# Attention and token-mixing MLP in one kernel: another tile for the fetched reciprocals, division in halves, fetches at other slots, one more raw weight block

## The chip, the cores and the metric

The kernel runs on one core of one Trainium2 chip. The metric is the device time of one execution in microseconds, as the median of several runs; lower is better. The profile is of one further execution, taken by the hardware profiler.

## What is computed

One input x (2048 tokens, 512 channels, float32) goes through two branches that a gate mixes.

```python
g = sigmoid((x * gate_w).sum(-1, keepdims=True))
# branch A: 32 heads of 16 channels
q, k, v = heads(x @ wqkv)
o = softmax(q @ k.T * 16**-0.5) @ v
a = merge(o) @ wo
# branch B: an MLP over the token axis, the same for every channel
h = layernorm(x)
u = gelu(einsum("bsd,sf->bdf", h, w1) + b1)       # F = 1792
b = einsum("bdf,fs->bds", u, w2) + b2             # transposed back to (tokens, channels)
out = g * a + (1 - g) * b
```

## The kernel before

**Precision.** Products are made of float32r parts: a matrix is split into a high part (a cast) and a low part (the difference), and three products are added (high by high, high by low, low by high). `split` (L66 the cast, L67 the subtraction) does this for weights, activations and the attention's result.

**First part, up to about 305 us.** Values, queries and keys are projected; q and k parts go to DRAM. Then comes the first layer of branch B, with w1 in blocks of 128 x 512. `load_weight` asks for a raw block on the SP queue (L132, tile `w_raw`, three buffers), and `split_weight` splits an earlier one. The second layer's blocks (w2) use the same tiles.

**Attention.** There are 32 *groups*: 16 pairs of heads, for the first half of the queries and then for the second. A group has 4 *slots* (the variable `two` counts all 128 of them), and a slot has 2 *phases*. In a phase TensorE makes 8 score products into PSUM banks (L830), ScalarE takes the exponentials (L850), and TensorE multiplies those of the phase before by the values (L788, 32 small matmuls). VectorE adds the result to the group's tile `ot` (L808), after which the bank is free again. `ot` holds for each head 16 rows of sums and one row with the sum of the exponentials.

**Work beside it.** The same phases carry 6 (at times 8) matmuls of other work (L894): the second layer of branch B, whose output rows L514 writes to DRAM, and the output projection by wo, in pieces. A table `dense` says which matmuls lie in which slot; a table `calls` says which functions are called at the start of a slot. Both are filled ahead of the loop (L694 to L711), with `at` as the slot that the schedule has reached.

**The way of a group's result.** After a group's last addition `store_sums` stores the 16 rows per head (L756, `o<-ot`, four stores), inverts the row of sums in two steps on VectorE (L762 a maximum, L763 a reciprocal), in place in `ot` until `open_end` has been called and afterwards in a tile `sums`, and stores the reciprocals (L769, `r<-...`). Once four groups are stored, `fetch_o` brings them back as one operand of 128 partitions: it reads the result into the low parts' tile (L614, `o_lo<-o`, 512 KB) and the reciprocals, each row repeated 16 times, into a tile `o_sum` (L615, `o_sum<-r`, 512 KB). Two slots later VectorE multiplies the two over all 1024 columns (L618) and, in the next free phase, splits the product into `o_hi` and `o_lo`. There are eight fetches: `fetch_o(0, 0..3)` for the first half of the queries, with `o_sum` (one buffer) in the pool `o_pool`, and `fetch_o(1, 0..3)`, with `o_sum` (one buffer) in the pool `end`.

**The list `slow`.** VectorE's work that has no fixed place stands in this list with the slot from which it may run. In each phase at most one entry is taken, ahead of the phase's scores.

**Output rows.** `project` multiplies a piece of the attention's result by wo. `load` (L632) reads the row that it is added to, one slot ahead; when the slot's matmuls end, L636 adds into it, and L656 (`out_dram<-row`) or L658 stores it. In slots 112 to 119 these are the final rows of the first half. In slots 120 to 127 they are `base` rows of the second half, which stay in place for the end.

**Last pair.** The last pair of heads doesn't go through DRAM. Its part of wo (`wq`) is read by four strided reads (L595) into a cleared tile `wq_raw` and split on VectorE, all from `open_end` at slot 112, the split from slot 117.

**Queues.** All these reads and stores are issued by SP, in program order. Each of them also waits until the one eight places ahead has landed, because eight semaphores are used in turn. The order inside attention is fixed by hand (`manual_schedule`); ahead of it a scheduler sets the order.

Of the kernel before, what the change touches and what calls it, by code (L numbers as in the profile page):

```python
# [10 lines left out]
F32 = mybir.dt.float32  # L11
# [4 lines left out]
ALU = mybir.AluOpType  # L16
AX = mybir.AxisListType
# [5 lines left out]
P = 128  # L23
S = 2048
D = 512
F = 1792
H = 32
DH = 16
# [3 lines left out]
NB = 512  # L32
# [23 lines left out]
LEAST_SUM = 1e-35  # L56
# [3 lines left out]
def gated_mix(ctx: ExitStack, tc: tile.TileContext, a_x, a_wqkv, a_wo, b_w1, b_b1, b_w2, b_b2, gate_w, out):  # L60
    nc = tc.nc
    xf, of = (t.rearrange("b s d -> (b s) d") for t in (a_x, out))

    def split(hi, lo, src, copy, sub):

        copy(hi, src)  # L66
        return sub(lo, src, hi.bitcast(F32), ALU.subtract)  # L67
# [15 lines left out]
    ident = const.tile([P, P], F32, name="ident")  # L83
# [17 lines left out]
    wk = wk_ctx.enter_context(tc.tile_pool(name="wk", bufs=3, side="right"))  # L101
# [19 lines left out]
    def load_weight():  # L121
        if blocks:
            src = blocks.pop(0)
            raw = wk.tile([P, NB], F32, name="w_raw", bufs=3)
            if len(src.shape) == 2:
                raw = raw[:, : src.shape[1]]
                dst = raw
            else:
                raw = raw[:, : src.shape[1] * P]
                dst = raw.rearrange("p (k s) -> p k s", s=P)  # L130
            with tc.issue_after(x_load.ins):
                nc.sync.dma_start(dst, src)  # L132
            loaded.append(raw)
# [281 lines left out]
    with tc.tile_pool(name="ln1", bufs=3, side="right") as ln, tc.tile_pool(name="gl", bufs=2, side="right") as gl:  # L415
# [29 lines left out]
        for f0, cs in order.items():  # L445
            n = min(NB, F - f0) // P
# [29 lines left out]
    o_pool = ctx.enter_context(tc.tile_pool(name="o", bufs=1, reuse_waits="tile"))  # L476
# [3 lines left out]
    QW = 2 * NB  # L480
# [64 lines left out]
    wq = []  # L545
# [30 lines left out]
    least = []  # L576
    rows = {}

    def open_end():

        nonlocal end, sums_of
        u_ctx.close()
        wk_ctx.close()
        end = end_ctx.enter_context(tc.tile_pool(name="end", bufs=1, side="right", reuse_waits="tile"))

        sums_of = end.tile([P, P], F32, name="sums_of")
        nc.vector.tensor_copy(
            sums_of.rearrange("p (j r) -> p j r", r=32),
            ident.rearrange("p (j r) -> p j r", r=32)[:, :, DH:VC].broadcast_to([P, P // 32, 32]),
        )  # L590
        wq.extend(end.tile([P, 2, D], F32R, name=f"wq{n}") for n in range(2))
        raw = end.tile([P, 2, D], F32, name="wq_raw")
        nc.gpsimd.memset(raw, 0.0)
        for j in range(4):
            nc.sync.dma_start(  # L595
                raw[32 * j : 32 * j + DH], a_wo[(H - 2) * DH : H * DH, :].rearrange("(i r) c -> r i c", i=2)
            )
        slow.append((two + 5, lambda: split(wq[0], wq[1], raw, nc.vector.tensor_copy, nc.vector.tensor_tensor)))

        least.append(end.tile([P, 1], F32, name="least"))  # L600
        nc.vector.tensor_reduce(least[0], ident.rearrange("p (j r) -> p j r", r=32)[:, :, DH], axis=AX.X, op=ALU.add)
        nc.vector.tensor_scalar(least[0], least[0], -1.0, 3e38, ALU.add, ALU.mult)
        nc.vector.tensor_scalar_add(least[0], least[0], LEAST_SUM)

    def fetch_o(half, k, pairs=4):

        n = pairs * 2
        assert stored.issuperset(half * NP + 4 * k + p for p in range(pairs))
        pool, name, bufs = (end, str(k), 1) if half else (o_pool, "", 2)
        rb = pool.tile([P, QW], F32, name="o_sum", bufs=1)[: n * DH]  # L610
        hi = pool.tile([P, QW], F32R, name=f"o_hi{name}", bufs=bufs)[: n * DH]
        lo = pool.tile([P, QW], F32R, name=f"o_lo{name}", bufs=bufs)[: n * DH]
        raw = lo.bitcast(F32)
        nc.sync.dma_start(raw, o_d[half][k][: n * DH])  # L614
        nc.sync.dma_start(rb, r_d[half][k][:n, None, :].broadcast_to([n, DH, QW]))  # L615

        at = two + (1 if two + 2 == NG * TWOS else 2)
        slow.append((at, lambda: nc.vector.tensor_mul(rb, raw, rb)))  # L618
# [59 lines left out]
    def call(at, *what):  # L678
        calls.setdefault(at, []).append(what)
# [397 lines left out]
```

## Time and profile before

| what | value |
|---|---|
| median of 3 runs | 1310.69 us (1309.16 to 1312.59) |
| profiled execution | 1314.28 us |
| its span, from the first to the last instruction | 1312.5 us |
| granted TensorE clock, mean | 0.99 |
| HBM traffic | 98.85 MB read, 35.78 MB written |

How to read the views that follow. The page gives the busy time of each engine. A table of stages gives, for stretches of time, the busy time of each engine with the number of instructions, the granted clock, the busy share of the 16 DMA engines and GB/s. A list of waits names who waited, at which line, for whom, with total, number and longest. A timeline row gives start, length, engine, line and operation, the tiles (output, then inputs), how many such instructions it merges, and in brackets the idle time before it with what ended it. The rows of an engine called SPq are the issues of transfers: their length is the time that issuing took, not the transfer. Rows of groups by form give count, busy us, mean ns and idle time before.

### The profile page before, as it was taken

What the parts mean: (1) busy time and instruction counts of PE and PEld (TensorE: products, weight loads), DVE (VectorE), ACT (ScalarE), POOL (GpSimd) and SP (SyncE); (2) the same over time, 40 slices, a digit from 0 to 9 for tenths busy, and PEclk for the clock granted to TensorE, in tenths of its full rate; (3) what the DMA queues carried; (4) which work ended last, traced back from release to release, by engine and by line L of the source; (5) the groups of instructions that cost most, each with busy time, mean ns of one, the idle gap of its engine ahead of it and who ended that gap; (6) DMA issues with size and microseconds to landing.
All of it is one profiled execution on the core that took longest, in us unless ns stands there. A gap on an engine that the chain in (4) does not pass through costs nothing.

```text
span 1312.5 us, 33002 instructions
## 1 busy us (share of the span) xinstructions
PE 1286.2 (98%) x13282; PEld 781.1 (60%) x13282; DVE 593.6 (45%) x1040; ACT 1088.3 (83%) x1504; POOL 206.4 (16%) x435
## 2 busy tenths in 40 slices
PE   9999999999999999999999999999999998989898
PEld 7888888885555555555555555555555554544455
DVE  5675371445444343444554433444334433545435
ACT  3443343447999999999999999999999997999794
POOL 0210244453111111110110011111111111000000
PEclk9999999999999999999999999999999998999899
DMA  4497643336333343444544433344433334465522
GB/s 129 136 316 269 226 113 98 99 92 137 70 90 59 81 87 69 82 79 87 109 92 121 94 68 76 78 77 83 74 66 70 74 62 101 75 144 129 121 64 73
DMA packets 92524, 136.86 MB, mean 104 GB/s; under 512 B 14197, under 2 KB 53259, under 8 KB 89292
## 3 DMA queue, kind: packets, MB, share of 16 engines
q1 hardware_dynamic: 91788, 133.63, 43.3%
q8 instruction: 106, 1.74, 0.6%
q10 hardware_dynamic: 576, 1.05, 0.2%
q14 instruction: 54, 0.44, 0.1%
HBM read 98.85 MB, written 35.78 MB: 103 GB/s over the span
## 4 chain that ended last, share of the span: by engine, by line
PE 94%; DMA 3%; DVE 2%; SPq 1%; issue 0%; ACT 0%; DVEq 0%
PE s L788 35%; PE s L830 22%; PE dn L894 14%; PE acc L413 12%; PE acc L74 10%; DMA row<-part 1%; PE pa L933 1%; DMA o<-ot 1%; PE acc L185 1%; DMA out_dram<-row 1%; PE acc L252 0%; DMA ks<-kp 0%; DVE ot L808 0%; PE acc L229 0%; SPq L499 0%
## 5 line engine op out<-in xcount | busy, mean ns | idle before, releaser
L850 ACT ACTIVATE pt<-s 128x1024 f32<-128x1024 f32 (+1 forms) x1280 | 960.3, 910 | 26.4 <-PE s L830 10.4
L830 PE MATMUL s<-qs,ks 64*128 64x512 f32 x2048 | 508.1, 422 | 7.2 <-DVE ot L808 4.2
L788 PE MATMUL s<-pt,v 128*17 128x256 f32 x8192 | 496.5, 383 | 0.0
L808 DVE TENSOR_TENSOR ot<-s,ot 128x256 f32<-128x256 f32 x476 | 202.8, 426 | 501.9 <-PE s L788 423.8
L830 PEld LDWEIGHTS s<-qs,ks 64*128 64x128 f32 x2048 | 301.7, 185 | 193.0 <-ACT pt L850 147.5
L788 PEld LDWEIGHTS s<-pt,v 128*17 128x17 f32 x8192 | 216.4, 98 | 247.7 <-ACT pt L850 87.5
L894 PE MATMUL dn<-u_hi,w_lo 64*128 64x512 f32 x430 | 178.3, 415 | 0.0
L894 PE MATMUL dn<-u_lo,w_hi 64*128 64x512 f32 x430 | 170.8, 397 | 0.0
L894 PE MATMUL dn<-u_hi,w_hi 64*128 64x512 f32 x428 | 168.8, 394 | 0.0
L67 POOL TENSOR_TENSOR w_lo<-w_raw,w_hi 128x512 fp32r<-128x512 f32 (+1 forms) x126 | 148.9, 1184 | 126.2 <-ACT w_hi L66 108.3
L898 POOL MEMSET token<- 1x1 f32 x256 | 22.8, 89 | 859.1 <-PE dn L894 835.9
L66 ACT CAST w_hi<-w_raw 128x512 fp32r<-128x512 f32 (+1 forms) x67 | 38.1, 569 | 80.2 <-PE acc L413 62.2
L763 DVE RECIPROCAL ot<-ot 128x256 f32<-128x256 f32 x54 | 94.7, 1753 | 1.8
L413 PE MATMUL acc<-h_hi,w_hi 128*128 128x512 f32 x224 | 87.1, 389 | 0.0
L413 PE MATMUL acc<-h_lo,w_hi 128*128 128x512 f32 x224 | 87.1, 389 | 0.0
L413 PE MATMUL acc<-h_hi,w_lo 128*128 128x512 f32 x224 | 87.1, 389 | 0.0
L894 PEld LDWEIGHTS dn<-u_lo,w_hi 64*128 64x128 f32 x430 | 79.4, 185 | 7.7
L894 PEld LDWEIGHTS dn<-u_hi,w_hi 64*128 64x128 f32 x428 | 79.7, 186 | 1.2
L894 PEld LDWEIGHTS dn<-u_hi,w_lo 64*128 64x128 f32 x430 | 79.5, 185 | 1.3
L894 PE MATMUL dn<-wo_hi,o_hi 64*128 64x512 f32 x112 | 46.4, 415 | 11.5 <-DVE row L636 11.5
L74 PE MATMUL acc<-xt_hi,wc_hi 128*128 128x512 f32 x128 | 49.8, 389 | 0.0
L74 PE MATMUL acc<-xt_lo,wc_hi 128*128 128x512 f32 x128 | 49.8, 389 | 0.0
(144 smaller groups left out, 1012.9 us busy)
## 6 DMA issues: line engine op xcount, KB each, us to landing
w_raw<-in_B_w_dram SPq DMA_DIRECT2D x96, 256.0 KB
ks<-kp SPq DMA_DIRECT2D x192, 128.0 KB
qs<-qp SPq DMA_DIRECT2D x256, 64.0 KB
qp<-pc SPq DMA_DIRECT2D x16, 768.0 KB
x<-in_A_x_dram SPq DMA_DIRECT2D x32, 256.0 KB
kp<-pc SPq DMA_DIRECT2D x16, 512.0 KB
w_raw<-in_B_w_dram SPq DMA_DIRECT2D x32, 128.0 KB
bp<-row SPq DMA_DIRECT2D x16, 256.0 KB
```

What stands on the lines that cost most here:

```text
L66: copy(hi, src)
L67: return sub(lo, src, hi.bitcast(F32), ALU.subtract)
L74: nc.tensor.matmul(ps, a, b, start=start and n == 0, stop=stop and n == last)
L185: nc.tensor.transpose(turns[t][:, k, :], xs[t][:, k * P : (k + 1) * P], ident)
L413: nc.tensor.matmul(p, a, b, start=first and k == 0, stop=last and k == 2)
L763: nc.vector.reciprocal(rt[:, cols], rt[:, cols])
L788: mm = nc.tensor.matmul(av[32 * j : 32 * j + VC, i * QC : (i + 1) * QC], v[:, c, g % NP * 2 + i, :], pt[:, h * QC : (h + 1) * QC], start=t ...
L808: reads(nc.vector.tensor_tensor(x, y, x, ALU.add), bank)
L830: mm = nc.tensor.matmul(banks[:, bank, :], kt[grp][rows, c * P : (c + 1) * P], qt[grp][rows, qb * NB : (qb + 1) * NB], start=True, stop=True,)
L850: act = nc.scalar.activation(dst, banks[:, at[0] : at[-1] + 1, :], AF.Exp, scale=SCALE)
L894: mm = nc.tensor.matmul(ps, a[half], b[half], start=first and not second, stop=last and bool(second))
L898: fence = nc.gpsimd.memset(token, 0.0)
```

## The change

1. `fetch_o` reads the reciprocals into the high parts' tile of the fetch instead of `o_sum`. The shared tile is no longer written by a transfer here.
2. The division is cut in two halves of 512 columns. Each is an entry of `slow` of its own and has a product, a cast and a subtraction through a 128 x 512 tile `o_sum` in `o_pool` (one buffer, also used by `load_wo`); `o_sum` in the pool `end` is gone.
3. Fetches are called at other slots: `fetch_o(0, 0)` at 41 instead of 42, `(0, 2)` at 101 instead of 104, `(0, 3)` at 105 instead of 107. The others stay (`(0, 1)` at 45, `(1, 0..3)` at 113, 115, 117 and 126).
4. The reads of `wq` and the clearing of its raw tile leave `open_end` for a function `load_wq`, called at slot 121 instead of 112; its split may run from slot 123 instead of 117.
5. `w_raw` has four buffers instead of three.

```diff
     def load_weight():
         if blocks:
             src = blocks.pop(0)
-            raw = wk.tile([P, NB], F32, name="w_raw", bufs=3)
+            raw = wk.tile([P, NB], F32, name="w_raw", bufs=4)
...
     def load_wo(k):
-        raw = o_pool.tile([P, QW], F32, name="o_sum")[:, :D]
+        raw = o_pool.tile([P, D], F32, name="o_sum")
...
+    def load_wq():
         wq.extend(end.tile([P, 2, D], F32R, name=f"wq{n}") for n in range(2))
         raw = end.tile([P, 2, D], F32, name="wq_raw")
         nc.gpsimd.memset(raw, 0.0)
...
-        slow.append((two + 5, lambda: split(wq[0], wq[1], raw, nc.vector.tensor_copy, nc.vector.tensor_tensor)))
+        slow.append((two + 2, lambda: split(wq[0], wq[1], raw, nc.vector.tensor_copy, nc.vector.tensor_tensor)))
...
         pool, name, bufs = (end, str(k), 1) if half else (o_pool, "", 2)
-        rb = pool.tile([P, QW], F32, name="o_sum", bufs=1)[: n * DH]
         hi = pool.tile([P, QW], F32R, name=f"o_hi{name}", bufs=bufs)[: n * DH]
         lo = pool.tile([P, QW], F32R, name=f"o_lo{name}", bufs=bufs)[: n * DH]
-        raw = lo.bitcast(F32)
+        raw, rb = lo.bitcast(F32), hi.bitcast(F32)
...
-        slow.append((at, lambda: nc.vector.tensor_mul(rb, raw, rb)))
-        slow.append((at, lambda: split(hi, lo, rb, nc.vector.tensor_copy, nc.vector.tensor_tensor)))
+
+        def divide(i):
+            cols = slice(i * NB, (i + 1) * NB)
+            o = o_pool.tile([P, NB], F32, name="o_sum")[: n * DH]
+            nc.vector.tensor_mul(o, raw[:, cols], rb[:, cols])
+            split(hi[:, cols], lo[:, cols], o, nc.vector.tensor_copy, nc.vector.tensor_tensor)
+
+        slow.extend((at, lambda i=i: divide(i)) for i in range(2))
...
-            call(at - 8, fetch_o, 0, 0)
+            call(at - 9, fetch_o, 0, 0)
...
-    call(at - 8, fetch_o, 0, 2)
-    call(at - 5, fetch_o, 0, 3)
+    call(at - 11, fetch_o, 0, 2)
+    call(at - 7, fetch_o, 0, 3)
     call(at, open_end)
+    call(at + 9, load_wq)
```

Behind the new function all lines of the changed kernel stand 7 or 8 higher (L614 and L615 become L615 and L616, L632 becomes L639, L756 becomes L764, L769 becomes L777).

The SP queue before, from the reciprocals of group 24 to the end of group 26's first reads (`qs` and `ks` are the query and key reads of the group that follows, `w_raw` a weight block, `bp` an output row of branch B):

```order
L769 DMA r_2708<-ot 2x1x256 x4
L499 DMA qs<-qp_62 16x1024 x8
L614 DMA o_lo<-o_2696 128x1024
L615 DMA o_sum<-r_2704 128x1x1024
L132 DMA w_raw<-in_B_w_dram 128x2x128
L756 DMA o_2700<-ot 16x2x256 x4
L499 DMA ks_2690<-kp_67 16x2048 x6
```

The same place of the SP queue now, from the key reads of the group before on:

```order
L499 DMA ks_2689<-kp_67 16x2048 x6
L615 DMA o_lo<-o_2696 128x1024
L616 DMA o_hi<-r_2704 128x1x1024
L132 DMA w_raw<-in_B_w_dram 128x4x128
L777 DMA r_2708<-ot 2x1x256 x4
L499 DMA qs<-qp_62 16x1024 x8
L132 DMA w_raw<-in_B_w_dram 128x2x128
L764 DMA o_2700<-ot 16x2x256 x4
L499 DMA ks_2690<-kp_67 16x2048 x6
L515 DMA bp_2678<-row 128x512
L615 DMA o_lo<-o_2697 128x1024
L616 DMA o_hi<-r_2705 128x1x1024
```

The fetch of `o_2696` moved from ahead of the four stores of `ot` to behind the key reads before, and the next fetch follows the key reads of group 26.

The SP queue before, in group 28, from its first query read to the row load behind the fetch at slot 113:

```order
L499 DMA qs<-qp_63 16x1024 x8
L595 DMA wq_raw<-in_A_wo_dram 16x2x512 x4
L632 DMA row<-part_2722 128x512
L756 DMA o_2700<-ot 16x2x256 x4
L499 DMA ks_2690<-kp_68 16x2048 x6
L656 DMA out_dram<-row 128x512
L614 DMA o_lo_13648<-o_2698 128x1024
L615 DMA o_sum<-r_2706 128x1x1024
L632 DMA row<-part_2723 128x512
```

The same place now:

```order
L499 DMA qs<-qp_63 16x1024 x8
L639 DMA row<-part_2722 128x512
L764 DMA o_2700<-ot 16x2x256 x4
L499 DMA ks_2690<-kp_68 16x2048 x6
L663 DMA out_dram<-row 128x512
L615 DMA o_lo_13655<-o_2698 128x1024
L616 DMA o_hi_13654<-r_2706 128x1x1024
L639 DMA row<-part_2723 128x512
```

The four reads of `wq_raw` are gone from here; the rest stands as it stood.

VectorE before, around the first fetch's division in groups 10 and 11:

```order
L66 CAST w_hi<-w_raw 128x512
L808 TENSOR_TENSOR ot<-s,ot 128x256
L808 TENSOR_TENSOR ot<-s,ot 64x256
L618 TENSOR_TENSOR o_sum<-o_lo,o_sum 128x1024
L808 TENSOR_TENSOR ot<-s,ot 128x256
L808 TENSOR_TENSOR ot<-s,ot 64x256
L66 CAST o_hi<-o_sum 128x1024
L67 TENSOR_TENSOR o_lo<-o_sum,o_hi 128x1024
```

The same place on VectorE now:

```order
L623 TENSOR_TENSOR o_sum<-o_lo,o_hi 128x512
L66 CAST o_hi<-o_sum 128x512
L67 TENSOR_TENSOR o_lo<-o_sum,o_hi 128x512
L816 TENSOR_TENSOR ot<-s,ot 128x256
L816 TENSOR_TENSOR ot<-s,ot 64x256
L66 CAST w_hi<-w_raw 128x512
L816 TENSOR_TENSOR ot<-s,ot 128x256
L816 TENSOR_TENSOR ot<-s,ot 64x256
L623 TENSOR_TENSOR o_sum<-o_lo,o_hi 128x512
L66 CAST o_hi<-o_sum 128x512
L67 TENSOR_TENSOR o_lo<-o_sum,o_hi 128x512
```

Two runs of three instructions stand where one and two stood, and the first of them comes ahead of a weight block's cast. TensorE's and ScalarE's instructions stay in the same order throughout.

More of the change, by code (lines that the diff above doesn't have):

```diff
@@ L590, in open_end @@
         )
+        least.append(end.tile([P, 1], F32, name="least"))
+        nc.vector.tensor_reduce(least[0], ident.rearrange("p (j r) -> p j r", r=32)[:, :, DH], axis=AX.X, op=ALU.add)
+        nc.vector.tensor_scalar(least[0], least[0], -1.0, 3e38, ALU.add, ALU.mult)
+        nc.vector.tensor_scalar_add(least[0], least[0], LEAST_SUM)
+    def load_wq():
         wq.extend(end.tile([P, 2, D], F32R, name=f"wq{n}") for n in range(2))
@@ L597, in open_end @@
             )
-        slow.append((two + 5, lambda: split(wq[0], wq[1], raw, nc.vector.tensor_copy, nc.vector.tensor_tensor)))
[L600 to L603, printed above, removed]
+        slow.append((two + 2, lambda: split(wq[0], wq[1], raw, nc.vector.tensor_copy, nc.vector.tensor_tensor)))
     def fetch_o(half, k, pairs=4):
```

## The prediction

> **What bounds the kernel now.** I read the page first, then a table of stages by group, then the waits of VectorE and of the SP queue, then both timelines at the places that stood out.
>
> ```profile
> PE 1286.2 (98%) x13282; PEld 781.1 (60%) x13282; DVE 593.6 (45%) x1040; ACT 1088.3 (83%) x1504; POOL 206.4 (16%) x435
> ```
>
> TensorE is busy 98% of the span, so what a change of waits can bring lies in the 26 us in which it is not (1312.5 less 1286.2), and in matmuls that run at a lowered clock behind a pause. A table by group shows where that is. Each of these stages holds the 256 matmuls of L788 of one group (8 phases of 32), so all should last alike; the columns are length, TensorE busy, weight loads busy, granted clock, DMA share and GB/s.
>
> ```profile
> 1031.90:1061.70 29.80, 15.37 (x256) 6.75 (x256) 1.00 0.43 82
> 1091.60:1128.50 36.90, 17.07 (x256) 7.06 (x256) 0.91 0.44 88
> 1128.50:1158.60 30.10, 15.37 (x256) 6.72 (x256) 1.00 0.35 72
> 1158.60:1193.90 35.30, 16.47 (x256) 6.98 (x256) 0.95 0.65 148
> 1193.90:1235.50 41.60, 16.46 (x256) 7.01 (x256) 0.88 0.53 125
> ```
>
> Group 24 takes 29.80 us: 3.73 a phase, 7.45 a slot. The four groups after 1091.6 take 36.90, 30.10, 35.30 and 41.60: 7.1, 0.3, 5.5 and 11.8 more, 24.7 in all. Some 0.2 of the last is the first phase with eight side products, so **24.5 us** are lost to waiting. With the loss comes a granted clock of 0.88 to 0.95. VectorE's waits between 1085 and 1235 say on what (total, times, longest):
>
> ```profile
> DVE row L636 <- DMA row<-part: 8.9, 2, 7.5
> DVE ot L762 <- DMA o<-ot: 6.2, 2, 5.2
> DVE row L636 <- DMA out_dram<-row: 5.9, 1, 5.9
> ```
>
> All are transfers. VectorE works in order, and behind each waiting instruction stands the addition L808 that gives a PSUM bank back to TensorE; so its wait is passed on. The SP timeline shows what stood ahead of those transfers. First the start of group 26 (start, length of issue, line, tiles), with VectorE's instruction that waited:
>
> ```profile
> 1087.88 0.42 SPq L614 DMA_DIRECT2D o_lo<-o  x1
> 1088.34 0.63 SPq L615 DMA_DIRECT2D o_sum<-r  x1
> 1089.08 0.40 SPq L132 DMA_DIRECT2D w_raw<-in_B_w_dram  x1
> 1090.40 1.78 SPq L756 DMA_DIRECT2D o<-ot  x4
> 1092.23 8.02 SPq L499 DMA_DIRECT2D ks<-kp  x6
> ```
>
> ```profile
> 1099.85 0.29 DVE L762 TENSOR_SCALAR ot<-ot 128x256 f32<-128x256 f32 x1 [5.19 <-DMA o<-ot]
> ```
>
> The fetch at slot 104 (two reads of 512 KB) is issued just ahead of the four stores o<-ot, and the inversion L762 overwrites the tile that these stores read. They were all issued by 1092.2 and let VectorE go at 1099.85. I call this place A. Next the row loads in groups 28 and 29:
>
> ```profile
> 1156.81 2.53 SPq L595 DMA_DIRECT2D wq_raw<-in_A_wo_dram  x4
> 1166.30 0.43 SPq L614 DMA_DIRECT2D o_lo<-o  x1
> 1166.77 0.63 SPq L615 DMA_DIRECT2D o_sum<-r  x1
> 1167.46 0.45 SPq L632 DMA_DIRECT2D row<-part  x1
> ...
> 1187.75 0.64 SPq L615 DMA_DIRECT2D o_sum<-r  x1
> 1188.49 0.40 SPq L632 DMA_DIRECT2D row<-part  x1
> ...
> 1204.52 0.43 SPq L614 DMA_DIRECT2D o_lo<-o  x1
> 1211.51 0.62 SPq L615 DMA_DIRECT2D o_sum<-r  x1
> 1212.18 0.46 SPq L632 DMA_DIRECT2D row<-part  x1
> ```
>
> ```profile
> 1178.76 0.75 DVE L636 SCALAR_TENSOR_TENSOR row<-dn,g,row 128x512 f32<-128x512 f32 x1 [5.92 <-DMA out_dram<-row]
> 1196.71 0.75 DVE L636 SCALAR_TENSOR_TENSOR row<-dn,g,row 128x512 f32<-128x512 f32 x1 [1.47 <-DMA row<-part]
> 1218.95 0.75 DVE L636 SCALAR_TENSOR_TENSOR row<-dn,g,row 128x512 f32<-128x512 f32 x1 [7.47 <-DMA row<-part]
> ```
>
> ```profile
> SPq L615 <- DVE o_lo L67: 18.7, 3, 7.3
> ```
>
> Place B: the row for slot 114 is asked for at 1167.46, behind a fetch, and read at 1178.76. (The wait is put down to out_dram<-row; the row load behind the fetch is what L636 needs.) Places C and D: the reciprocals' read L615 has to wait until VectorE has split the fetch before, since all of them use one tile (18.7 us in three waits), and SP holds the row load behind it: at D the fetch starts at 1204.52, the row load leaves at 1212.18, and the row is there at 1218.95.
>
> **The change part by part.** *Reciprocals into the high parts' tile.* The wait of L615 goes, since each fetch has a high tile of its own. At D the row load then leaves 7.0 us earlier (1211.51 less 1204.52), at C as much, as the same wait stood there. C lost 1.5 us (its row's 1.47) and is covered by 7.0: gone. The third wait delayed the q and k reads of group 28 and lies in the 0.3 of group 27: gone too.
>
> *Fetch at slot 101 in place of 104, 105 in place of 107.* The fetch now follows the k reads, and the stores o<-ot stand ahead of these, not behind the fetch. A loses its cause: 7.1 us. What stands behind the fetch now is a weight block, asked for blocks ahead of its use, and the stores of the reciprocals, which nothing reads for several groups. The fetch at slot 42 already leaves at that point of the queue:
>
> ```profile
> 616.03 0.67 SPq L615 DMA_DIRECT2D o_sum<-r  x1
> ...
> 637.60 1.23 DVE L618 TENSOR_TENSOR o_sum<-o_lo,o_sum 128x1024 f32<-128x1024 f32 x1
> ```
>
> SP runs ahead there, so calling it at slot 41 moves nothing on SP; only the division comes a slot earlier, near 637.60 - 7.45 = 630.1. At B the read issued at 1166.77 was done by 1178.76, when the row behind it was read, so within 12.0 us; the one at 616.03 is then there by 628.0. The cover is 2.1 us; below it this costs nothing.
>
> *The wq reads go from slot 112 to 121.* This takes 2.53 us of issue out of the queue ahead of B's row load, and up to 3.4 if I follow the later issues through, since the k reads ahead of the fetch then start sooner and finish sooner. Where they go, they stand ahead of base rows, which are asked for one slot (7.45) before use: 0, at worst 2.5. The memset of wq_raw moves with them on GpSimd, which is 16% busy: 0.
>
> What is left at B follows from two additions L808, the last undisturbed one and the one that came late:
>
> ```profile
> 1171.96 0.88 DVE L808 TENSOR_TENSOR ot<-s,ot 128x256 f32<-128x256 f32 x2 [2.83 <-PE s L788]
> ...
> 1179.43 0.87 DVE L808 TENSOR_TENSOR ot<-s,ot 128x256 f32<-128x256 f32 x2
> ```
>
> Undisturbed, it would start at 1171.96 + 3.73 = 1175.69; it came 3.74 late and group 28 lost 5.5, a factor of 1.5 by the lowered clock. With the row 2.5 to 3.4 us sooner, L636 starts between 1175.4 and 1176.2, and L808 0.75 later: 0.5 to 1.3 late. That costs 0.5 to 2.0; I take **0.9**. D's row load has the same queue ahead of it (stores, six k reads, a row store, the fetch), now without the wait, so I take **0.9** for D in place of 10.1 (11.8 less C's 1.5 and the 0.2).
>
> *Division in halves.* The forms of VectorE's work, now and in the size to come:
>
> ```profile
> L618 DVE TENSOR_TENSOR o_sum<-o_lo,o_sum 128x1024 f32<-128x1024 f32 x7 | 8.6, 1226 | 0.2
> L67 DVE TENSOR_TENSOR o_lo<-o_sum,o_hi 128x1024 fp32r<-128x1024 f32 x7 | 8.6, 1225 | 0.2
> L66 DVE CAST o_hi<-o_sum 128x1024 fp32r<-128x1024 f32 x7 | 4.9, 695 | 0.2
> L67 DVE TENSOR_TENSOR wo_lo<-o_sum,wo_hi 128x512 fp32r<-128x512 f32 x3 | 2.1, 694 | 0.1
> L66 DVE CAST wo_hi<-o_sum 128x512 fp32r<-128x512 f32 x3 | 1.3, 428 | 0.1
> ```
>
> Now 1.23 in one phase and 0.70 + 1.23 = 1.92 in another, 3.15 a fetch. Then twice 0.69 + 0.43 + 0.69 = 1.81 (the product priced as the subtraction of that size), 3.63: half a microsecond more per fetch, 3.8 over eight. A phase with a half, a row (0.75) and two additions (0.88) holds 3.44 of 3.73. VectorE is 45% busy, so nothing of it is on the path: 0. In a phase without that room it would cost 0.5 at most.
>
> *Fourth raw block.* SP waits long for a free raw block, but in a stage that TensorE bounds:
>
> ```profile
> SPq L132 <- POOL w_lo L67: 130.5, 72, 4.9
> ```
>
> ```profile
> 296.00:312.00 16.00, 13.15 (x73) 9.05 (x75) 14.48 (x17) 10.81 (x17) 7.32 (x7) 0.94 0.77 166
> ```
>
> TensorE's idle time at the turn to attention, 2.85 us, is all that an earlier block could shorten, and I allow as much the other way; I take 0.
>
> **Sum.** 24.5 lost now, less 0.9 + 0.9 left, less 0.2 for small shifts: **22.5 us** saved. The profiled execution (1314.28, span 1312.5) would come to 1291.8. It ran 3.6 above the median of the three runs; I take the same saving from that: 1310.69 - 22.5 = **1288.2 us**.
>
> **The rivals.** *First: the rows stay late behind the replicated read.* The fetch itself is as large as before, and B's row load still leaves right behind it. If the row still comes some 5 us late there, B keeps its 5.5, and D, freed of the wait, becomes a second B at 5.5: saved 7.1 + 0.3 + 1.5 + (10.1 - 5.5) = 13.5, so **1297.2**. For it speaks that a row asked for at 1212.18 came 6.8 us later though nothing but the reciprocals' read was just ahead; against it, that it can only keep what the wq reads did not cause, and they are gone from B's queue. The DMA share while such a read ran almost alone:
>
> ```profile
> 623.50:626.50 3.00, 3.00 (x44) 1.64 (x44) 0.85 (x2) 3.00 (x5) 0.09 (x1) 1.00 0.54 118
> ```
>
> It is about half, so the read seems to use half of the engines and hold back what needs all of them. The Trainium skill (page "DMA: Bandwidth & Descriptors", section "Why a DMA increments its semaphore by 16 and not by 1") says that a copy runs on the largest number of engines up to 16 that divides the slowest dimension on both sides, which for 8 source rows gives 8; by that rule another target tile does not shorten the read, and the time goes toward this rival's. The share of 0.54 agrees. Chance 0.13.
>
> *Second, the slower side: the earlier division waits for its reads.* VectorE would stop in front of L808, as at A. It decides from reads that land 2.1 us later than the 12.0 above; a half of 1.81 beside 0.88 leaves another 1.0 in the phase. To lose all of 22.5 and 3.9 more over eight fetches, each must wait 3.3: reads that take 18.4 us, for **1315**. No read here was that late, and DMA share in these groups is 0.35 to 0.65. Chance 0.02.
>
> *Third: the change doesn't do what it says,* because the reads, in a tile of their own, meet another wait (of the fetch for the tile's last reader), and A's stores queue behind something else: about **1310**. Against it: the high tiles' readers ended dozens of slots before, or never were. Chance 0.03.
>
> **How the numbers follow.** The forecast has 0.80, the first rival 0.13, the second 0.02, the third 0.03, the rest is spread. The low end is all of 24.5 saved, with 1.7 for the runs' own spread: 1284.5. The high end takes in the first rival: 1297.5. A measurement here can tell about 0.3% (3.9 us) from no change; faster by more than that: forecast, first rival and a part of the rest, 0.94; same 0.03; slower 0.03.
>
> **What would show it.** In the profile after: groups 26 to 29 at 30 us each in the same table; no wait of L762 on o<-ot over 1 us; no wait of SP on VectorE's split; the row load of group 29 within 1 us of its fetch; granted clock 1.00 between 1060 and 1240. The two waits of L636 that may stay, at slots 114 and 118, under 2 us. I am wrong if one of those groups is still over 33 us, or if the multiplications that divide are preceded by a wait on a DMA.

## The result, and the profile after

The changed kernel takes **1287.53 us** (median of 4 runs, 1286.65 to 1288.42), the kernel before 1310.76 beside it (4 runs, 1309.16 to 1312.59). The ratio is 0.9822, with a 95% interval of 0.9805 to 0.9839. That is 23.2 us less; the forecast was 1288.2, from 22.5 us.

A word on line numbers: the change adds eight lines, so the addition L808 is now L816, the multiplication by the values L788 is L796, the inversion L762 is L770, the output row's L636 is L643, its load L632 is L639, and the reciprocals' read L615 is L616. The rows meant at B, C and D are those of slots 114, 116 and 118, final rows of the first half; the expectations call them base rows. The profiled execution took 1286.96 us, its span 1285.2. Its first line:

```profile
PE 1276.1 (99%) x13282; PEld 777.0 (60%) x13282; DVE 596.4 (46%) x1064; ACT 1087.2 (85%) x1504; POOL 208.9 (16%) x435
```

TensorE's idle time is 9.1 us (1285.2 less 1276.1) where it was 26.3. The table by group, here for groups 24 and 26 to 29 (length, then the busy time of the matmuls of L796 and of their weight loads alone, granted clock, DMA share, GB/s; all tables of groups below have these columns):

```profile
1027.70:1057.50 29.80, 15.37 (x256) 6.74 (x256) 1.00 0.42 81
1087.40:1117.20 29.80, 15.37 (x256) 6.73 (x256) 1.00 0.42 94
1117.20:1147.10 29.90, 15.37 (x256) 6.72 (x256) 1.00 0.33 69
1147.10:1177.00 29.90, 15.37 (x256) 6.70 (x256) 1.00 0.76 186
1177.00:1208.20 31.20, 15.37 (x256) 6.72 (x256) 1.00 0.64 153
```

The last four rows were 36.90, 30.10, 35.30 and 41.60 and are now 29.80, 29.90, 29.90 and 31.20: 143.9 has become 120.8, **23.1 us less**, and the clock is 1.00 in all of them. Group 24 also ends 4.2 us earlier than it did (1057.50 against 1061.70); that part comes from the turn to attention, near 300 us (undo_raw, below). The two together, 27.3, are the whole difference of the profiled executions (1314.28 less 1286.96). The medians differ by 4.1 less, since the profiled execution of before was 3.5 above its median and that of after 0.6 below.

VectorE's waits between 1080 and 1212 (total, times, longest) no longer have a transfer of any size; the two rows that answer to those of before:

```profile
DVE row L643 <- PE s L796: 5.1, 2, 2.9
DVE ot L770 <- DMA o<-ot: 0.6, 2, 0.5
```

The wait for the stores o<-ot was 6.2 and is 0.6. The row of L643 now names TensorE, for which VectorE may wait at no cost; but it hides something. SP and VectorE at place D (the row of slot 118), in the SP timeline and in VectorE's:

```profile
1182.38 0.43 SPq L615 DMA_DIRECT2D o_lo<-o  x1
...
1183.52 0.46 SPq L639 DMA_DIRECT2D row<-part  x1
```

```profile
1190.77 0.88 DVE L816 TENSOR_TENSOR ot<-s,ot 128x256 f32<-128x256 f32 x2 [0.93 <-PE s L796]
1194.51 0.75 DVE L643 SCALAR_TENSOR_TENSOR row<-dn,g,row 128x512 f32<-128x512 f32 x1 [2.85 <-PE s L796]
```

The fetch is issued without a gap, and the row load leaves 1.14 us after the fetch began, where it was 7.66 before (1204.52 to 1212.18). L643 starts at 1194.51. To be in time for an L816 at 1190.77 + 3.73 = 1194.50 it had to start 0.75 earlier; so it is still 0.76 late, and its row, asked for at 1183.52, has been 11 us on its way. The wait is put down to TensorE. That it is the row's is shown twice: by the trace's records of landings, in which the replicated read ahead of the row has landed at 1194.02 and the row at 1194.43, 0.08 before L643 starts, and by an experiment (rows_first).

### The profile page after: what moved, and what is told of

It is laid out like the page before. It is cut to its first block, busy times and chain, and to the rows that moved or that the text cites. A ratio compares the mean times of both kernels' runs of the same rounds, so it can differ in the third digit from the quotient of the medians.

```text
span 1285.2 us, 33027 instructions
## 1 busy us (share of the span) xinstructions
PE 1276.1 (99%) x13282; PEld 777.0 (60%) x13282; DVE 596.4 (46%) x1064; ACT 1087.2 (85%) x1504; POOL 208.9 (16%) x435
## 3 DMA queue, kind: packets, MB, share of 16 engines
q8 instruction: 106, 1.74, 0.6%
## 4 chain that ended last, share of the span: by engine, by line
PE 98%; ACT 0%; issue 0%; DVE 0%; DMA 0%; SPq 0%; DVEq 0%
PE s L796 37%; PE s L838 24%; PE dn L902 14%; PE acc L413 12%; PE acc L74 10%; PE pa L941 1%; PE acc L185 1%; PE dn L827 0%; PE acc L252 0%; ACT pt L858 0%; PE pa L971 0%; DMA wv_raw<-in_A_wqkv_dram 0%; DVE row L643 0%; DVE base L984 0%; DVE xt_lo L67 0%
## 5 line engine op out<-in xcount | busy, mean ns | idle before, releaser
L796 PE MATMUL s<-pt,v 128*17 128x256 f32 x8192 | 491.7, 380 | 0.0
L816 DVE TENSOR_TENSOR ot<-s,ot 128x256 f32<-128x256 f32 x476 | 202.8, 426 | 487.8 <-PE s L796 410.1
L796 PEld LDWEIGHTS s<-pt,v 128*17 128x17 f32 x8192 | 215.2, 97 | 243.3 <-ACT pt L858 87.7
L74 PE MATMUL acc<-xt_hi,wc_lo 128*128 128x512 f32 x128 | 49.8, 389 | 0.0
```

Of the source, the lines that this page charges most:

```text
L74: nc.tensor.matmul(ps, a, b, start=start and n == 0, stop=stop and n == last)
L796: mm = nc.tensor.matmul(av[32 * j : 32 * j + VC, i * QC : (i + 1) * QC], v[:, c, g % NP * 2 + i, :], pt[:, h * QC : (h + 1) * QC], start=t ...
L816: reads(nc.vector.tensor_tensor(x, y, x, ALU.add), bank)
```

## The experiments

The theory is the prediction's: the loss comes from what stands in SP's queue ahead of the stores (place A) and of the output rows (B, C, D), and each part of the change takes one such thing away. Its rivals: the replicated read keeps the rows late by itself; and parts of the change that don't matter. First each part alone, on the kernel before; then each part undone, on the changed kernel; then the order alone; then the read itself. The division in halves has no run of its own.

### One part alone, on the kernel before

**Only the slots of the first half's fetches.**

```diff
-            call(at - 8, fetch_o, 0, 0)
+            call(at - 9, fetch_o, 0, 0)
-    call(at - 8, fetch_o, 0, 2)
-    call(at - 5, fetch_o, 0, 3)
+    call(at - 11, fetch_o, 0, 2)
+    call(at - 7, fetch_o, 0, 3)
```

> The kernel before with the three fetches at their new slots (41, 101, 105) and nothing else. My theory: place A is the four stores of ot queued behind the fetch at slot 104, so group 26 falls from 36.9 to 30 us and group 27 from 30.1 to 29.8; B, C and D stay (groups 28 and 29 at 35.3 and 41.6). 1310.7 - 7.4 = 1303.3 us. Rival, the stores are late because the queue is full at any slot: group 26 stays at 36 to 37 or group 25 takes over its loss, 1310 us.

Measured: 1302.43 us (1302.06 to 1302.98), before beside it 1310.13; ratio 0.9938 (0.9914 to 0.9962). Groups 26, 28 and 29:

```profile
1090.10:1120.00 29.90, 15.37 (x256) 6.73 (x256) 1.00 0.41 94
...
1149.80:1181.90 32.10, 15.37 (x256) 6.71 (x256) 1.00 0.67 163
1181.90:1223.50 41.60, 16.23 (x256) 6.92 (x256) 0.92 0.53 126
```

Group 26 is at 29.9: A is gone, by moving fetches alone; of the three, the one from slot 104 stood ahead of the four stores. Group 29 keeps its 41.6. Group 28 loses only 2.3 here, where it lost 5.5 in the kernel before: the row of slot 114 is late by another amount from profile to profile. The addition behind it comes 2.14 us late here (1169.43 less 1163.56 + 3.73), and came 3.74 late there.

**Only the tile** (reciprocals into the high parts' tile). The product goes into a tile `o_sum` of `o_pool`; it and the split still go over all 1024 columns at once, so this run does not hold the halves.

```diff
-        rb = pool.tile([P, QW], F32, name="o_sum", bufs=1)[: n * DH]
-        raw = lo.bitcast(F32)
+        raw, rb = lo.bitcast(F32), hi.bitcast(F32)
...
-        slow.append((at, lambda: nc.vector.tensor_mul(rb, raw, rb)))
-        slow.append((at, lambda: split(hi, lo, rb, nc.vector.tensor_copy, nc.vector.tensor_tensor)))
+        o = o_pool.tile([P, QW], F32, name="o_sum")[: n * DH]
+        slow.append((at, lambda: nc.vector.tensor_mul(o, raw, rb)))
+        slow.append((at, lambda: split(hi, lo, o, nc.vector.tensor_copy, nc.vector.tensor_tensor)))
```

> The kernel before with the reciprocals read into the high parts' tile, the product made over all 1024 columns in a tile that only VectorE uses, old slots, old place of the wq reads, three raw blocks. My theory: the wait of the reciprocals' read on VectorE's split goes; C (1.5 us) and 9.2 of D's 10.1 go, and the 0.3 of group 27; A (7.1) and B (5.5) stay. 1310.7 - 11.0 = 1299.7 us; group 28 at 35, group 29 at 31. Rival, the row stays late behind the replicated read itself: D becomes a second B (5.5 left), 1310.7 - 6.4 = 1304.3 us, group 29 at 35 to 36.

Measured: 1297.65 us (1297.22 to 1299.26); ratio 0.9905 (0.988 to 0.9929). Groups 26, 28 and 29:

```profile
1089.10:1124.90 35.80, 16.56 (x256) 7.00 (x256) 0.95 0.41 93
...
1154.70:1188.30 33.60, 17.01 (x256) 7.09 (x256) 0.95 0.70 175
1188.30:1219.00 30.70, 15.37 (x256) 6.72 (x256) 1.00 0.64 151
```

Group 29 goes from 41.6 to 30.7 while A and B stay. The first rival gave D 5.5 us in this kernel, so a group of about 35; it is refuted there. In group 28 the addition comes 2.04 us late (1173.93 less 1168.16 + 3.73), and the group loses 3.8.

**Only the wq reads** (slot 121, in a function of their own).

```diff
     call(at, open_end)
+    call(at + 9, load_wq)
```

> The kernel before with the wq reads at slot 121 and their split from slot 123, nothing else. My theory: the row load of slot 114 leaves 2.5 to 3.4 us sooner and B falls from 5.5 to 0.9; A, C and D stay. 1310.7 - 4.6 = 1306.1 us, group 28 at 30.7. Rival, the row stays late behind the replicated read: group 28 stays at 35, 1310.7 us.

Measured: 1304.44 us (1303.54 to 1304.83); ratio 0.9954 (0.9936 to 0.9971). Groups 28 and 29:

```profile
1156.20:1187.00 30.80, 15.36 (x260) 6.70 (x264) 1.00 0.72 164
1187.00:1225.90 38.90, 16.98 (x260) 7.08 (x264) 0.91 0.57 137
```

B falls to 1.0 us, against the 0.9 of the prediction. Group 29 falls by 2.7 as well, which no theory had said: wq's division into parts also left slot 117, VectorE reached the split of the fetch sooner, and the reciprocals' read that waits for that split could leave sooner: it leaves 3.5 us after its fetch began (1197.06 to 1200.57), where it left 7.0 after (1204.52 to 1211.51).

### One part undone, on the changed kernel

**Three raw weight blocks in place of four.**

```diff
-            raw = wk.tile([P, NB], F32, name="w_raw", bufs=4)
+            raw = wk.tile([P, NB], F32, name="w_raw", bufs=3)
```

> The changed kernel with three raw weight blocks instead of four. My theory: the fourth block changes nothing that TensorE waits for, 1287.5 us, within 1 us. Rival: the 4.2 us that the profile after has less at the turn to attention (TensorE idle 0.8 instead of 2.9 us between 296 and 312, clock 1.00 instead of 0.94, first phase 3.74 instead of 4.65) come from the block that is loaded earlier; then 1291.7 us, and the table of that stage looks as before.

Measured: 1289.70 us (1289.11 to 1290.39, 5 runs); ratio to before 0.9843 (0.9822 to 0.9863). It is 2.2 us above the changed kernel, so the forecast's 0 was wrong. The turn to attention, first in the changed kernel, then with three blocks (length, then busy time of TensorE, weight loads, VectorE, ScalarE and GpSimd, clock, DMA share, GB/s):

```profile
296.00:312.00 16.00, 15.17 (x109) 10.19 (x108) 13.30 (x18) 12.83 (x21) 7.25 (x6) 1.00 0.82 170
```

```profile
296.00:312.00 16.00, 13.20 (x92) 9.17 (x93) 14.78 (x17) 11.19 (x18) 6.93 (x7) 1.00 0.75 166
```

SP's first q reads of the attention, again the changed kernel first, and then TensorE's longest wait with three blocks:

```profile
296.07 5.91 SPq L499 DMA_DIRECT2D qs<-qp  x8
```

```profile
296.20 0.37 SPq L132 DMA_DIRECT2D w_raw<-in_B_w_dram  x1
...
298.23 5.06 SPq L499 DMA_DIRECT2D qs<-qp  x8
```

```profile
PE s L838 <- DMA qs<-qp: 1.5, 1, 1.5
```

With three blocks a weight block is still ahead of the first q reads at 296.20, having waited for its tile, and the q reads leave later: 298.23 in place of 296.07, 2.2 us. TensorE's idle time in the stretch grows from 0.83 to 2.80 us, 1.5 of it spent waiting for them, and the time is 2.2 longer. It is the same mechanism as at B and D: a load that can wait holds one that can't. This is half of the 4.2 us by which the profiles differ at the turn: group 26 begins at 1089.5 with three blocks, at 1087.4 with four and at 1091.6 in the kernel before. The other half goes with the clock, which is 0.94 in this stretch in the profile before and 1.00 here; no part of the change is shown to bring it.

**The old slots.** The diff is that of the slots above, the other way round.

> The changed kernel with the three fetches of the first half back at their old slots (42, 104, 107). Theory: the fetch at slot 104 is ahead of the stores o<-ot again, the inversion L762 (here L770) waits for them and group 26 lasts 36 to 37 us instead of 29.8; the other groups stay. Time 1287.5 + 7.1 = 1294.6 (1293 to 1296). Rival, that the place of the fetch no longer matters once the reads have a tile of their own: 1287.5.

Measured: 1293.27 us (1291.75 to 1295.66); ratio 0.9865 (0.9849 to 0.988). Group 26 and its inversion:

```profile
1089.00:1126.40 37.40, 17.07 (x256) 7.08 (x256) 0.91 0.40 90
```

```profile
1097.73 0.29 DVE L770 TENSOR_SCALAR ot<-ot 128x256 f32<-128x256 f32 x1 [5.60 <-DMA o<-ot]
```

A is back, though each read now has its own tile: its cause is the order in the queue. The median is 5.7 above the changed kernel's, while the group is 7.6 longer: the runs scatter by 4, the profiled one is the longest of them (1295.66), and the two profiles are not alike elsewhere (group 29 is 0.6 shorter here).

**One shared tile for the reciprocals of the second half.** Slots, halves, wq and raw blocks stay.

```diff
         raw, rb = lo.bitcast(F32), hi.bitcast(F32)
+        if half:
+            rb = end.tile([P, QW], F32, name="r_rep", bufs=1)[: n * DH]
```

> The changed kernel, but the four fetches of the second half read their reciprocals into one shared tile again (the division in halves, the slots, the wq move and the fourth raw block stay). Theory (the wait of SP for VectorE's division is the cause at C and D): SP waits in front of the reciprocals' reads of the second and third fetch; the wait is shorter than before, since the division's products in the shared tile are done with after two halves, but the row for slot 118 comes some 6 us later than in the changed kernel; group 29 lasts 38 to 41 us, time about 1296 (1293 to 1298). Rival (the replicated read itself holds the row up): no difference, 1287.5.

Measured: 1293.88 us (1292.85 to 1295.36); ratio 0.987 (0.9855 to 0.9886). Group 29, the second fetch's reciprocals and the row load in SP's timeline, and the row's use:

```profile
1178.00:1216.90 38.90, 16.73 (x256) 7.05 (x256) 0.91 0.57 132
```

```profile
1190.26 0.62 SPq L618 DMA_DIRECT2D r_rep<-r  x1
1190.93 0.46 SPq L641 DMA_DIRECT2D row<-part  x1
```

```profile
1200.27 0.75 DVE L645 SCALAR_TENSOR_TENSOR row<-dn,g,row 128x512 f32<-128x512 f32 x1 [7.03 <-issue]
```

The row load leaves at 1190.93, 7.4 us later than in the changed kernel (6.4 later if one counts from the start of the group), and L645 waits 7.03: the shared tile alone brings the late row load and the long group back. SP waited 7.2 us for VectorE ahead of the reciprocals' reads of the second and third fetch; the q and k reads between those two fetches were issued later too (by 1187.4, against 1181.9). The replicated read is the same in both kernels, so it is not the cause of these 7.7 us (38.9 less 31.2).

**The wq reads at slot 112 again.** The diff is that of the wq reads, the other way round.

> The changed kernel with the wq reads back at slot 112 (and their split back at its old distance). Theory: the row for slot 114 comes 2.5 to 3.4 us later; group 28 lasts 32 to 35 us, group 29 stays at 30 to 31; time 1289.5 to 1292.5. Rival, that the wq move brought nothing once the rest of the queue is free: 1287.5.

Measured: 1292.04 us (1289.52 to 1292.7); ratio 0.9853 (0.9836 to 0.9869). Group 28 and the row of slot 114:

```profile
1148.50:1182.60 34.10, 15.50 (x256) 6.67 (x256) 0.95 0.72 175
```

```profile
1161.75 0.88 DVE L816 TENSOR_TENSOR ot<-s,ot 128x256 f32<-128x256 f32 x2 [2.83 <-PE s L796]
1167.66 0.75 DVE L643 SCALAR_TENSOR_TENSOR row<-dn,g,row 128x512 f32<-128x512 f32 x1 [5.03 <-DMA row<-part]
1168.32 0.87 DVE L816 TENSOR_TENSOR ot<-s,ot 128x256 f32<-128x256 f32 x2
```

B is back with 4.2 us. L816 comes 2.84 late (1168.32 less 1161.75 + 3.73), and the group loses 1.4 more than that, with a clock of 0.95. That is again the factor of 1.5 which the prediction took from the kernel before; the last section shows that it is no factor.

### The order alone

**Row loads ahead of the fetches,** in the changed kernel.

```diff
-    for k, n in enumerate((1, 3, 5)):
-        call(at + n, fetch_o, 1, k)
+    start = at
     at = put_outputs(range(NH), 6, 12, at)
+    for k, n in enumerate((1, 3, 5)):
+        call(start + n, fetch_o, 1, k)
```

> The changed kernel with the base-row loads issued ahead of the fetches at slots 113, 115 and 117 (nothing else moved). Theory: the two rows that are still late (slots 114 and 118; phases 3.9 and 4.5 us long instead of 3.73) come in time, L643 no longer waits, and 0.9 us goes: 1286.6 (1286 to 1287.3). Rival: the fetch, one load later, makes the division wait, or the loss there was not the row's: 1287.5 or above.

Measured: 1286.56 us (1285.82 to 1287.78, 5 runs); ratio 0.9818 (0.9804 to 0.9832). The medians differ by 1.0, where 0.9 was expected, but the intervals overlap almost wholly, so the time alone doesn't tell it from the changed kernel. The profile does, in groups 28 and 29:

```profile
1148.50:1178.40 29.90, 15.35 (x260) 6.68 (x264) 1.00 0.70 184
1178.40:1208.70 30.30, 15.40 (x260) 6.74 (x264) 1.00 0.61 150
```

Group 29 is at 30.3 in place of 31.2, and the 5.1 us of L643's wait "for TensorE" at slots 114 and 118 are gone. So that wait was the row's. What L643 still waits there, at most 0.9 us at a time, is for the product itself.

**The same, with the wq reads at slot 112.**

```diff
-    call(at + 9, load_wq)
+    call(at, load_wq)
```

> The changed kernel with the base-row loads ahead of the fetches and the wq reads back at slot 112. Theory (the wq reads cost time only through the row of slot 114, which they and the fetch push back together): with the row ahead of its fetch it has 6 us or so more, group 28 stays at 29.9 to 30.5 and the time is 1286.6 to 1287.6; so the wq move is worth nothing in that order. Rival (the wq reads alone make that row late): group 28 at 32 to 34, 1289 to 1291.

Measured: 1288.11 us (1287.95 to 1288.27, 5 runs), before beside it 1312.15; ratio 0.9815 (0.9802 to 0.9828). The ratio is that of rows_first (0.9818) within the intervals. Group 28:

```profile
1147.70:1177.50 29.80, 15.37 (x256) 6.74 (x256) 1.00 0.74 197
```

With the rows first, the wq move, worth 4.5 us in the changed kernel (1292.04 less 1287.53), is worth nothing that the runs can tell.

**Order only, on the kernel before:** the new slots of the first half and the rows ahead of the fetches; the shared tile, the whole-tile division, wq at slot 112 and three raw blocks stay. The diff is the one of the slots and the one of the rows.

> The kernel before with calls moved and nothing else: the first half's fetches at the changed kernel's slots (41, 101, 105), and the base-row loads of slots 114, 116 and 118 issued ahead of the fetches instead of behind them. The shared o_sum, the whole-tile division, three raw blocks and the wq reads at slot 112 stay. Theory (what the late rows and stores lost was their place in SP's queue): the waits of L615 for the split stay, but no row is behind them; A, C and D go, B goes or keeps up to 1; against 1310 some 22 to 24 less: 1286 to 1289. Rival: the waits of L615 hold the next thing on SP (the next group's q and k reads, the rows' stores), or the wq reads alone make B's row late: 1292 to 1298.

Measured: 1293.32 us (1292.32 to 1293.66); ratio 0.9881 (0.9864 to 0.9897). That is not the theory's time: A and B are gone (groups 26 to 28 at 29.9, 29.8 and 29.9), and at C no row is waited for, but group 29 is still long. The row of slot 118, the third fetch on SP, and VectorE:

```profile
1178.80:1215.50 36.70, 17.06 (x256) 7.05 (x256) 0.91 0.61 149
```

```profile
1189.27 0.43 SPq L632 DMA_DIRECT2D row<-part  x1
...
1195.07 0.62 SPq L615 DMA_DIRECT2D o_sum<-r  x1
```

```profile
1193.82 1.23 DVE L67 TENSOR_TENSOR o_lo<-o_sum,o_hi 128x1024 fp32r<-128x1024 f32 x1
1195.60 0.75 DVE L636 SCALAR_TENSOR_TENSOR row<-dn,g,row 128x512 f32<-128x512 f32 x1 [0.56 <-DMA row<-part]
...
1202.31 1.23 DVE L618 TENSOR_TENSOR o_sum<-o_lo,o_sum 128x1024 f32<-128x1024 f32 x1 [5.17 <-DMA o_sum<-r]
```

The row is now in time (0.56). But the reciprocals' read still leaves only when the split before it has ended (1193.82 + 1.23 = 1195.05), at 1195.07, and the division of that fetch stands in VectorE's order ahead of an addition (L809 in this kernel): it waits 5.17 us, and with it the bank. The time is in the rival's interval, but its cause was in neither expectation. The tile of its own is needed for the division's sake too.

### The replicated read

**In two reads of four rows.**

```diff
-        nc.sync.dma_start(rb, r_d[half][k][:n, None, :].broadcast_to([n, DH, QW]))
+        for s in range(0, n, 4):
+            e = min(s + 4, n)
+            part = slice(s * DH, e * DH)
+            nc.sync.dma_start(rb[part], r_d[half][k][s:e, None, :].broadcast_to([e - s, DH, QW]))
```

> The changed kernel with each replicated read of the reciprocals issued as two reads of four rows (the last as four and two), the same bytes to the same places. If a replicated read runs on as many engines as it has source rows, each half takes as long as the whole did and one after the other they take twice as long, or they run side by side on different engines and take the same; theory for the first case: the rows behind it at slots 114 and 118 come 2 to 6 us later, 1290 to 1296, with a DMA share near 0.3 where a read runs alone. If the source rows don't set the engines: the row comes 0.5 later (one more issue), 1287.5 to 1288.5, with a DMA share near 0.54 as before.

**As a plain read of the same size** (of o, a second time; the division then has the wrong divisor).

```diff
-        nc.sync.dma_start(rb, r_d[half][k][:n, None, :].broadcast_to([n, DH, QW]))
+        nc.sync.dma_start(rb, o_d[half][k][: n * DH])
```

> The changed kernel with the replicated read of the reciprocals replaced by a second plain read of o of the same size into the same tile; the division then uses the wrong divisor, so the output isn't the reference's. If it is the replication that keeps half of the engines idle and the rows late: DMA share near 1 where such a read runs alone, the phases of the rows of slots 114 and 118 go from 3.9 and 4.5 to 3.73, time 1286.6. If any read of 512 KB behaves so: share near 0.54 and time 1287.5.

Measured: 1293.18 us (1292.34 to 1296.88), ratio 0.9889 (0.9868 to 0.9911), for the two reads; 1286.65 us (1286.13 to 1287.09), ratio 0.9833 (0.9817 to 0.985), for the plain one. Where the read at slot 41 runs nearly alone, in the changed kernel and then with two reads (the last two columns are DMA share and GB/s):

```profile
619.00:622.00 3.00, 3.00 (x44) 1.47 (x42) 0.67 (x2) 3.00 (x5) 0.09 (x1) 1.00 0.51 116
```

```profile
619.00:622.00 3.00, 3.00 (x44) 1.48 (x42) 0.68 (x2) 3.00 (x5) 0.09 (x1) 1.00 0.25 79
```

Eight source rows, half of the engines; four, a quarter: the trace's records of packets show 8 in flight at once there, and 4. The plain read lands at 619.74 us, the replicated one at 623.57. While the two reads of the fetch ran, both plain here:

```profile
617.00:618.50 1.50, 1.50 (x22) 0.72 (x14) 0.75 (x3) 1.50 (x3) 0.00 (x0) 1.00 1.04 415
```

All engines, with 16 packets in flight. The rule of the Trainium skill that the prediction weighed (page "DMA: Bandwidth & Descriptors", section "Why a DMA increments its semaphore by 16 and not by 1"), that the number of engines follows from the slowest dimension, agrees with the three shares 0.51, 0.25 and 1.04. What it makes of the rows, first groups 28 and 29 with two reads, then with the plain read:

```profile
1147.10:1179.00 31.90, 15.37 (x256) 6.73 (x256) 1.00 0.65 168
1179.00:1214.80 35.80, 16.00 (x256) 6.86 (x256) 0.95 0.51 133
```

```profile
1147.70:1177.50 29.80, 15.37 (x256) 6.70 (x256) 1.00 0.69 188
1177.50:1207.90 30.40, 15.37 (x256) 6.70 (x256) 1.00 0.58 152
```

With four rows the output rows are late at both places again, and the groups are 2.0 and 4.6 us longer than in the changed kernel; with a plain read neither row is late. So the first rival's mechanism is real: a replicated read does hold up the row behind it. The records of landings show it in both kernels. At D the row lands at 1194.43 behind the replicated read's 1194.02 in the changed kernel and at 1218.88 behind 1218.46 in the kernel before; at B at 1163.86 behind 1163.44, and at 1178.64 behind 1177.83. In the changed kernel there is just enough time in front of the row for it to cost 1.0 and not 11.

## Why the prediction was right, point by point

- **A, 7.1 us: right.** Alone it gave 7.7 (only_slots, with the small share of group 27), and undoing it made group 26 7.6 longer (5.7 by the medians).
- **C and D by the shared tile: right.** The wait of SP for the split went, the row load left 1.14 us after the fetch began, and D fell from 10.1 to 0.9 (group 29, 31.2 less the 30.3 of rows_first). Taken away alone (only_tile) and put back alone (undo_tile) it did what was said. The prediction did not see that the shared tile has a second path to the end: with the rows out of the way (order_only), it makes the division late.
- **B by the wq reads: right.** 0.9 was forecast, 1.0 measured for the part alone. In the changed kernel about 0.1 is left (group 28 at 29.9), and together with D 1.0, where the sum had 1.8. A wait that the profile names for TensorE was the row's (rows_first).
- **Division in halves, 0: right as far as the profile shows.** No run changes the halves alone. In the changed kernel's profile groups 10, 11, 25 and 26, in which the fetches of the first half are divided, last 29.8 to 29.9 us, like group 24, and no multiplication that divides waits for a DMA.
- **Fourth raw block, 0: the term that was mis-sized; it is 2.2 us.** The prediction allowed up to 2.85, saw the idle time of TensorE at the turn, and took 0 without following SP's queue there. The row that would have told it is the first q read behind the weight blocks.
- **The first rival** (1297.2) has its mechanism, but not its price: in this order of the queue the read costs the rows 1.0 us and not 11 (5.5 at each of two places). **The second,** the division that waits for its reads, did not occur in the changed kernel and did in order_only, where it cost 6.8 us (36.7 less 29.9). **The third** did not occur.
- **The signs.** Three fell short: the row load of group 29 left 1.14 us after its fetch began and not within 1, the two waits that might stay, at slots 114 and 118, were 2.2 and 2.9 us and not under 2 (the profile puts them down to TensorE), and group 29 is at 31.2 and not at 30. The others came.
- **The sum.** 22.5 forecast, 23.2 measured by the medians. In it 2.2 for the raw block were missing, and 0.8 too much was left for B and D; together these would make 25.5. The remaining 2.3 isn't located. The base of 24.5 us is one profile, 3.6 us above the median to which the saving was applied, in which each of the three places A, B and D had a lowered clock as well; how much a place loses by that differs between profiles of the same lateness (last section). So the nearness to 0.7 us is in part luck.

The parts alone gave 7.7, 12.5 and 5.7, and the raw block 2.2, which is 28.1, more than the whole. For one thing, wq's move took 2.7 of D, which the tile takes too; for another, B lost less in the kernels of one part than in the kernel before (2.3 and 3.8 against 5.5), though neither changes the order ahead of that row. Between these two the difference, 1.5 us, is the clock, shown below. In the kernel before the row itself came later: it landed 20.0 us after the start of its group (1178.64 less 1158.60), against 18.8 and 18.4, each time just behind the replicated read. Why that read took 11.1 us from its issue there, against 10.1 and 10.4, stays open.

## What to carry to other kernels

A queue in order is a place like an engine: when a small load is late, read what was issued ahead of it and ask of each whether it could go behind. Here the cheapest remedy, issuing the row first, makes another one (the wq move) worthless; but it doesn't replace the tile of its own, since a read that waits for its tile is late for its own use too. And a wait's releaser in the profile is only the last event that it could see: move the suspect, and see whether the wait goes.

## What the runs showed of the hardware

The 512 KB read that repeats eight source rows 16 times runs on half of the DMA engines (0.51) at 116 GB/s, four rows on a quarter (0.25) at 79 GB/s. Plain reads of that size run on all of them (1.04, 415 GB/s), and the row load asked for behind them comes in time. A load on all engines behind a replicated read ends with it: of the 16 landings that the trace records for the row asked for at 1183.52, eight came by 1192.38 and eight from 1194.09 to 1194.43, behind the read's last at 1194.02. So the row took 10.9 us, and the wait for it grows with two reads on a quarter of the engines and is gone with a plain one.

The factor of 1.5 between a late addition and what the group loses is no factor: it is the clock, and whether it falls isn't settled by the pause alone. At place B TensorE paused for 1.81 us in only_slots and for 1.74 in only_tile. TensorE's first matmul behind the pause and the next 32 of L788, first in only_slots, then in only_tile:

```profile
1169.66 0.47 PE L894 MATMUL dn<-wo_hi,o_hi 64*128 64x512 f32 x1 [1.81 <-DVE row L636]
...
1171.21 1.92 PE L788 MATMUL s<-pt,v 128*17 128x256 f32 x32
```

```profile
1174.16 0.47 PE L894 MATMUL dn<-wo_hi,o_hi 64*128 64x512 f32 x1 [1.74 <-DVE row L636]
...
1175.72 3.56 PE L788 MATMUL s<-pt,v 128*17 128x256 f32 x32
```

The 32 matmuls take 1.92 in the one and 3.56 in the other. The traces also record when the granted clock changes. In nine of the fourteen profiles (before and after counted) it falls to 0.50 ahead of the last work. Each time it stays there for 3.41, 6.83 or 10.24 us, that is one, two or three times 3.41, and within a trace all these stretches begin on one grid of 3.41 us. Cut by that grid, two stretches of only_slots and then two of only_tile (length, then busy time of TensorE, weight loads, VectorE, ScalarE, GpSimd, clock, DMA share, GB/s):

```profile
1165.40:1168.81 3.41, 2.44 (x35) 1.00 (x27) 0.05 (x1) 3.38 (x5) 0.09 (x1) 1.00 0.67 183
1168.81:1172.23 3.42, 2.57 (x31) 1.78 (x35) 2.69 (x4) 1.81 (x2) 0.09 (x1) 1.00 0.57 165
```

```profile
1172.26:1175.67 3.41, 1.67 (x12) 1.17 (x11) 2.35 (x4) 1.84 (x4) 0.00 (x0) 1.00 0.46 168
1175.67:1179.08 3.41, 3.41 (x33) 1.20 (x32) 0.39 (x1) 2.22 (x3) 0.09 (x1) 0.50 0.94 246
```

In only_slots the grid divides the pause into 0.97 and 0.85 us (3.41 less 2.44, 3.42 less 2.57), and the clock stays at 1.00. In only_tile the whole pause lies in one stretch, and the next one runs at 0.50. So additions that came 2.14 and 2.04 us late cost group 28 2.3 and 3.8. The Trainium skill (page "TensorE: Matmul & The Clock Gate", section "Part 1: The HAM clock gate (the "warmup" mystery)") says that the clock follows TensorE's activity in windows of about 3.4 us that run freely. That would make the same pause cheap or dear by where it falls in a window; these two profiles agree with it, but no run here moved a pause on purpose. So the price of a pause of 1.8 us is 2.3 or 3.8 here, and a small change far away can turn the one into the other.
